# Layer-normalised tokens of two blocks turned by VectorE and DRAM instead of TensorE, in an attention-plus-GLU kernel

## The chip, the core and the metric

The kernel runs on one core of one Trainium2 chip. The core has a matrix engine (TensorE, PE in the profile, with its weight loads in a row of their own, PEld), a vector engine (VectorE, DVE), an activation engine (ScalarE, ACT), a general engine (GpSimd, POOL), and a queue engine (SyncE, SP) that here does nothing but issue DMA transfers. POOL issues a few transfers too. The metric is the time of one execution on the device in microseconds; the kernel before takes 676.23 us, the median of three executions (675.65 to 677.13).

## The reference

A layer normalisation feeds two branches, whose results are added to the input. One branch is attention with a compressive memory over four segments of 512 tokens, the other a gated feed-forward network. All is float32; there are 2048 tokens of 448 features, 16 heads of 28 features, and 1792 hidden units.

```python
xn = _layernorm(x, axis=-1)
return x + _A_ref(xn, A_wq, A_wk, A_wv, A_wo, A_beta) + _B_ref(xn, B_w_gate, B_w_up, B_w_down)

# _A_ref: q, k, v from xn; then, segment by segment (N = 4, L = 512)
logits = einsum("bhqd,bhkd->bhqk", qs, ks) * scale + mask
a_dot = einsum("bhqk,bhkd->bhqd", softmax(logits), vs)
pq = where(qs > 0, qs + 1, exp(qs))              # the same map of ks gives pk
a_mem = einsum("bhld,bhde->bhle", pq, M) / (einsum("bhld,bhd->bhl", pq, z)[..., None] + 1e-6)
o = g * a_mem + (1.0 - g) * a_dot                # g = sigmoid(beta), per head
M = M + einsum("bhld,bhle->bhde", pk, vs);  z = z + einsum("bhld->bhd", pk)
# then o @ wo
# _B_ref: (sigmoid(x @ w_gate) * (x @ w_up)) @ w_down
```

## The kernel before

**Blocks and parts.** The tokens are worked in four blocks `b` = 0 to 3 of 512 (`L`), each of four tiles `t` of 128 tokens. `acc[b]` holds a block's input as loaded, 128 tokens on the partitions, and later the sum that becomes the output. For the matrix products the normalised tokens are needed the other way round, features on the partitions: `xs[b]`, seven chunks of 512 tokens. To keep float32 accuracy on a faster number format, each operand is split in a rounded part (chunks 0 to 3 of `xs`) and what rounding left (chunks 4 to 6, and the upper 64 partitions of chunk 3, since 448 features fill three and a half chunks of 128). A product of two such operands is 11 matmuls, listed by chunk in `TERMS`.

**The front** is the first part of the program, about 155 us of it, and the only part in which the change moves compute work. For each block it makes values (`values`, four times 11 matmuls, into `pv`), then seven column groups `k` = 0 to 6 of keys and queries (`keys_queries`, 11 matmuls each into `pp`), which ACT copies and rounds, DVE subtracts (`qk`) and SP stores to DRAM (`qd`). Some groups also get their feature map (`e`, by ACT and DVE). At `k` = 2 to 5 the keys' feature maps are turned by PE (`key_rows`, into `pk`) and copied by ACT to `kn`; after `k` = 6 the memory is updated (`update`, into `pmm`). From block 2 on the memory is also recalled (`recall`, into four banks `n2`, by products with `phi`, which SP loads), turned back and divided by DVE (`answer`), and stored through POOL's queue (`od`).

**The next block's tokens** are prepared in between. `statistics` (DVE) and `root` (ACT, a square root, whose function table ACT has to load) give mean and scale; `normalise` (line 343, DVE) writes a tile to `xn`, and POOL copies its last 64 columns once more (line 351), so that the half chunk can serve for both parts; `turn` (line 354) has PE turn the tile by four matmuls against the identity (line 103, into a PSUM bank `pt`), ACT round it into `xs` (line 105), and DVE subtract (lines 110 and 111). Block 1's tiles are turned at `k` = 3 to 6 of block 0, and the tiles of blocks 2 and 3 at `k` = 1 to 4 of the block before. The token blocks 2 and 3 are loaded by SP, each in one transfer, during blocks 0 and 1 (line 588).

**What sets the order.** In the front the order on PE, ACT and DVE is that in which the code is written. SP and POOL are ordered by a planner in the front; every queue runs strictly in its order, so a transfer that waits holds back those behind it. The PSUM banks also set limits: `pp` alternates between two pairs of banks, the values use the pair `p` that the even groups of `pp` use, and a bank is free again when ACT and DVE have read it. From the end of the front on, the feed-forward network, the softmax attention and the output projection are woven into one PE stream in a fixed order (`MANUAL`), with `acc[b]` receiving the feed-forward results (`pd`).

## Time and profile before

The profile is of one execution, which took 674.82 us; its span, from the first instruction to the end of the last, is 673.0 us, so 1.82 us lie around it.

| | before |
|---|---|
| median of three executions | 676.23 us |
| the profiled execution | 674.82 us |
| its span | 673.0 us |
| PE busy | 666.4 us (99%) |
| DVE busy | 565.8 us (84%) |
| ACT busy | 338.3 us (50%) |
| POOL busy | 141.9 us (21%) |
| PE's share of the chain that ended last | 96% |
| granted TensorE clock | 1.00 |

How to read it: a "busy" time counts the moments in which an engine had at least one instruction at work. Matmuls are pipelined, so the duration of one (about 0.39 us for 128x512) is longer than the step from one to the next. The chain follows the program back from its last instruction, at each step to what released it, and gives each piece the time by which it moved the chain on; a stretch of four matmuls there is their real price. An instruction row in an answer by time has its start, the time that it or the merged run of its kind took, the engine and the line, and in brackets how long the engine had been idle and for what.

### The profile page before, as it was taken

How to read it: one execution, taken by the hardware profiler on the slowest of the kernel's cores; microseconds unless marked ns; L12 is line 12 of the kernel's file. 1: busy time of each engine (PE TensorE's matmuls, PEld its weight loads, DVE VectorE, ACT ScalarE, POOL GpSimd, SP SyncE). 2: the span in 40 equal slices, each digit the busy share in tenths (PEclk: the TensorE clock that was granted, in tenths of full speed). 3: DMA queues.
4: the chain of work that ended last, by engine and by line, in shares of the span. 5: the costliest groups of instructions: out<-in, count | busy, mean ns of one | idle time of the engine just before them, and what ended most of it. 6: DMA issues, size and time to landing. Idle time of an engine off the chain costs nothing.

```text
span 673.0 us, 11207 instructions
## 1 busy us (share of the span) xinstructions
PE 666.4 (99%) x3954; PEld 555.8 (83%) x3954; DVE 565.8 (84%) x987; ACT 338.3 (50%) x563; POOL 141.9 (21%) x346
## 2 busy tenths in 40 slices
PE   8999999999999999999999999999999999999997
PEld 7888878778878888887887888788787887888897
DVE  6765686668999899899998899899998998999864
ACT  5846564524455464555644555464545554545320
POOL 3500010002212222232221212222222221321000
PEclk9999999999999999999999999999999999999999
DMA  7446658894423234323346322425342332423342
GB/s 273 176 163 250 204 224 259 299 298 148 127 57 102 59 110 106 85 74 89 72 77 134 94 72 57 103 57 138 79 102 57 98 89 70 99 78 79 96 166 100
DMA packets 45919, 84.42 MB, mean 125 GB/s; under 512 B 6312, under 2 KB 20520, under 8 KB 45352
## 3 DMA queue, kind: packets, MB, share of 16 engines
q1 hardware_dynamic: 42712, 76.26, 38.2%
q0 software_dynamic: 3008, 7.34, 5.1%
q8 instruction: 31, 0.51, 0.3%
q14 instruction: 24, 0.20, 0.1%
q10 hardware_dynamic: 144, 0.11, 0.0%
HBM read 51.05 MB, written 32.64 MB: 124 GB/s over the span
## 4 chain that ended last, share of the span: by engine, by line
PE 96%; DVE 2%; issue 1%; ACT 1%; DMA 0%; DVEq 0%
PE pgu L255 42%; PE pd L181 20%; PE pp L380 10%; PE st L658 6%; PE pa L744 5%; PE po L843 5%; PE pv L360 4%; PE pt L103 1%; PE pk L402 1%; PE n L435 0%; DVE e L392 0%; PE pmm L413 0%; DMA acc<-in_x 0%; DVE stats L319 0%; DVE xn L345 0%
## 5 line engine op out<-in xcount | busy, mean ns | idle before, releaser
L255 PE MATMUL pgu<-xs,wgu 128*128 128x512 f32 x1232 | 301.3, 392 | 0.0
L255 PEld LDWEIGHTS pgu<-xs,wgu 128*128 128x128 f32 x1232 | 228.7, 188 | 46.7 <-issue 2.5
L181 PE MATMUL pd<-wdn,hh 128*128 128x448 f32 x672 | 155.3, 366 | 0.0
L181 PEld LDWEIGHTS pd<-wdn,hh 128*128 128x128 f32 x672 | 122.7, 188 | 11.6 <-issue 0.8
L673 POOL TENSOR_SCALAR_AFFINE_SELECT w<-w 128x256 f32<-128x256 f32 (+1 forms) x160 | 76.8, 483 | 217.8 <-ACT w L662 151.5
L726 ACT ACTIVATE w<-w 128x1024 f32<-128x1024 f32 (+1 forms) x96 | 87.9, 915 | 58.2 <-DVE w L722 58.2
L662 ACT ACTIVATE w<-st 128x512 f32<-128x512 f32 x128 | 75.6, 592 | 56.7 <-PE st L658 52.3
L722 DVE TENSOR_TENSOR w<-w,mb 128x1024 f32<-128x1024 f32 (+1 forms) x96 | 100.4, 1053 | 0.8
L680 DVE TRANSPOSE_TENSOR_REDUCE mx<-w 128x32 f32<-128x1024 f32 x64 | 78.9, 1233 | 4.0 <-POOL w L673 4.0
L380 PE MATMUL pp<-xs,wqk 128*128 128x512 f32 x308 | 75.8, 395 | 0.2 <-DVE kn L441 0.2
L278 ACT ACTIVATE hh<-sg 128x512 fp32r<-128x512 f32 x56 | 35.4, 631 | 71.6 <-DVE sg L272 50.3
L183 DVE TENSOR_TENSOR acc<-pd,acc 128x448 f32<-128x448 f32 x112 | 67.4, 602 | 4.0 <-PE pd L181 4.0
L380 PEld LDWEIGHTS pp<-xs,wqk 128*128 128x128 f32 x308 | 56.6, 188 | 12.6 <-issue 0.8
L658 PE MATMUL st<-qk 84*128 84x128 f32 (+3 forms) x256 | 62.0, 313 | 0.0
L658 PEld LDWEIGHTS st<-qk 84*128 84x128 f32 x256 | 47.9, 189 | 8.7 <-issue 1.4
L262 ACT ACTIVATE sg<-pgu 128x512 f32<-128x512 f32 x56 | 33.2, 592 | 40.8 <-PE pgu L255 40.8
L387 DVE TENSOR_TENSOR qk<-pp,qk 128x512 fp32r<-128x512 f32 x28 | 19.3, 689 | 32.8 <-ACT e L385 29.9
L272 DVE SCALAR_TENSOR_TENSOR sg<-sg,pgu 128x512 f32<-128x512 f32 x56 | 37.7, 673 | 9.3 <-PE pgu L255 9.3
L708 DVE STREAM_TRANSPOSE mb<-top 128x1024 f32<-128x1024 f32 x32 | 39.5, 1235 | 3.3 <-POOL top L705 3.2
L360 PE MATMUL pv<-wv,xs 128*128 128x448 f32 x176 | 37.7, 368 | 0.9 <-DVE e L392 0.5
L281 DVE SCALAR_TENSOR_TENSOR hh<-sg,hh 128x512 fp32r<-128x512 f32 x56 | 38.2, 682 | 0.3 <-ACT hh L278 0.3
L744 PE MATMUL pa<-w,vv 128*32 128x128 f32 (+3 forms) x512 | 37.8, 436 | 0.0
(100 smaller groups left out, 604.8 us busy)
## 6 DMA issues: line engine op xcount, KB each, us to landing
qk<-qd SPq DMA_DIRECT2D x192, 112.0 KB
qd<-qk SPq DMA_DIRECT2D x28, 512.0 KB
raw<-in_w_ffn SPq DMA_DIRECT2D x14, 512.0 KB
vd<-vst SPq DMA_DIRECT2D x4, 1024.0 KB
vv<-vd SPq DMA_DIRECT2D x16, 256.0 KB
od<-w POOLq DMA_DIRECT2D x16, 256.0 KB, 4.1
sums<-od SPq DMA_DIRECT2D x32, 128.0 KB
out<-acc SPq DMA_DIRECT2D x15, 224.0 KB
```

The source lines that it names most:

```text
L181: T.matmul(pd[:, :D], l, r, start=n == 0, stop=n == len(mms) - 1)
L183: V.tensor_add(acc[b][:, t, :], pd[:, :D], acc[b][:, t, :])
L255: T.matmul(dst, wgu[f][:, w, side * P:(side + 1) * P], xs[b][:, a, :], start=n == 0, stop=n == len(TERMS) - 1)
L360: T.matmul(pv[:, :D], xs[b][:, a, t * P:(t + 1) * P], wv[w], start=n == 0, stop=n == len(TERMS) - 1)
L380: T.matmul(pp, wqk[c][:, w, :], xs[b][:, a, :], start=n == 0, stop=n == len(TERMS) - 1)
L658: T.matmul(st[:, at:at + L - kb * P], self.qk[:KS, 1, h, kb * P:(kb + 1) * P], self.qk[:KS, 0, h, kb * P:], start=True, stop=True)
L662: A.activation(w, st, AF.Copy)
L673: G.affine_select(d, d, pattern=pattern, base=0, channel_multiplier=-1, compare_op=ALU.is_ge, fill=MASK)
L680: V.tensor_reduce(self.mx[:, 32 * h:32 * h + 32], w3[:, h, :2 * L].rearrange("p (b n) -> p b n", n=32), axis=mybir.AxisListType.X, op=ALU. ...
L722: V.tensor_sub(w, w, m)
L726: A.activation(w, w, AF.Exp, scale=SCALE)
L744: T.matmul(pa[32 * j:32 * j + 32, kb * P:], self.vv[:, kb, 32 * j:32 * j + 32], self.pairs[j // 2].block(j % 2, kb), start=kb == 0, stop=k ...
```

## The change

In blocks 2 and 3 PE no longer turns the tokens; blocks 0 and 1 stay as they were. The tokens of blocks 2 and 3 are loaded in another layout (`load_strips`): a strip of 32 partitions takes 128 neighbouring tokens, so that partition 32q + r of tile t holds token 128q + 32t + r. After `normalise`, DVE turns each tile in squares of 32 by 32 (`V.transpose`) into a stage, which is the memory of `phi` for block 2 and that of `acc[2]` for block 3. Then (`spread`) four SP transfers write the stage to a new DRAM tensor `xd[b]`, features by tokens, in runs of 128 tokens (512 bytes); POOL issues two transfers that read it back, three full chunks straight into `xs[b]` chunks 4 to 6, and the last 64 features into a tile `tail`. `split_strips` finally makes the two parts in SBUF: ACT rounds and DVE subtracts, a chunk at a time at `k` = 2 to 5 of the block before, where PE's turned tiles were split.

The work also moves in time. Block 2's strips are loaded right behind the first weights, block 3's after the first key group of block 0. Block 2's statistics are now taken before block 0's key groups, its first tile is normalised at `k` = 5 of block 0, its other three while PE makes block 1's values. Block 3's statistics follow there, and its four tiles are normalised at `k` = 0 to 3 of block 1. Because `acc[2]` and `acc[3]` then hold strips or a stage, both blocks are loaded once more in their old layout at the start of the feed-forward network. POOL's copy of the 64 columns is left out for blocks 2 and 3.

PE in block 1, around its key groups `k` = 1 to 4 (`pp`, 11 matmuls each); `pk` are the key rows, `pt` the turned tokens. Before:

```order
L380 MATMUL pp<-xs_66,wqk_115 128x512 x11
L103 MATMUL pt<-ident,xn 128x128 x4
L380 MATMUL pp<-xs_66,wqk_116 128x512 x11
L402 MATMUL pk<-ident,e 128x128 x4
L103 MATMUL pt<-ident,xn 128x128 x4
L380 MATMUL pp<-xs_66,wqk_117 128x512 x11
L402 MATMUL pk<-ident,e 128x128 x4
L103 MATMUL pt<-ident,xn 128x128 x4
L380 MATMUL pp<-xs_66,wqk_118 128x512 x11
```

And now:

```order
L415 MATMUL pp<-xs_66,wqk_119 128x512 x11
L415 MATMUL pp<-xs_66,wqk_120 128x512 x11
L437 MATMUL pk<-ident,e 128x128 x4
L415 MATMUL pp<-xs_66,wqk_121 128x512 x11
L437 MATMUL pk<-ident,e 128x128 x4
L415 MATMUL pp<-xs_66,wqk_122 128x512 x11
```

The fours of `pt` are gone, and nothing has come in their place; block 2 reads the same, and the rest of PE's order is as it was.

DVE at the end of block 0 and while PE makes block 1's values (`qk` is the subtraction of key group 6, `mst` the memory's update, `xs_66` block 1's last tile; `acc_71` is block 2, `phi` its stage). Now:

```order
L353 TENSOR_SCALAR xn<-acc_71,mv_348,y_520 128x16x7x4
L362 STREAM_TRANSPOSE phi<-xn 128x14x32
L422 TENSOR_TENSOR qk<-pp,qk 128x512
L455 COPY mst_126<-pmm 28x128 x4
L110 TENSOR_TENSOR xs_66<-pt,xs_66 128x3x128
L111 TENSOR_TENSOR xs_66<-pt,xs_66 64x128
L353 TENSOR_SCALAR xn<-acc_71,mv_348,y_520 128x16x7x4
L362 STREAM_TRANSPOSE phi<-xn 128x14x32
```

Before, the two rows ahead of `qk` and the two at the end were not there; block 2's statistics stood at the end, and its normalisation came later.

POOL around its last weight splits (`wqk`, the seven key and query weights) and its copies of 64 columns (`xn`). Before:

```order
L479 TENSOR_TENSOR wqk_119<-wqk_raw,wqk_119 128x512
L351 COPY xn<-xn 128x64
L479 TENSOR_TENSOR wqk_120<-wqk_raw,wqk_120 128x512
L351 COPY xn<-xn 128x64 x9
```

And now:

```order
L515 TENSOR_TENSOR wqk_123<-wqk_raw,wqk_123 128x512
L515 TENSOR_TENSOR wqk_124<-wqk_raw,wqk_124 128x512
L359 COPY xn<-xn 128x64 x4
L376 DMA xs_67<-xd_93 128x3x512
L378 DMA tail<-xd_93 64x512
```

The first copy, for block 1's first tile, has moved behind the last weight's split (wqk_120 before, wqk_124 now); the eight copies for blocks 2 and 3 are gone, and the read of block 2's turned tokens (xs_67, tail) follows.

The diff:

```diff
@@ -116,6 +116,11 @@
     def x_block(b):
         return x[b * L:(b + 1) * L, :].rearrange("(t p) d -> p t d", p=P)
 
+    def load_strips(b):
+        for q in range(4):
+            nc.sync.dma_start(acc[b][32 * q:32 * q + 32],
+                              x[b * L + q * P:b * L + (q + 1) * P, :].rearrange("(t r) d -> r t d", r=32))
+
     ps = ctx.enter_context(tc.tile_pool(name="psum", bufs=1, space=PSUM))
 
     banks = {"p": 2, "s": 2, "m": 1, "gu": 2, "pd": 1}
@@ -147,6 +152,7 @@
     qd = [dram.tile([2 * D, 2, L], F32, name=f"qd{b}") for b in range(NB)]
     fd = [dram.tile([D, L], F32, name=f"fd{b}") for b in range(NB)]
     vd = [dram.tile([P, NT, H * 32], F32, name=f"vd{b}") for b in range(NB)]
+    xd = [dram.tile([D, L], F32, name=f"xd{b}") for b in range(NB)]
     od = [dram.tile([H * 32, L], F32, name=f"od{b}") for b in range(NB)]
 
     mid = ctx.enter_context(tc.tile_pool(name="mid", bufs=3, reuse_waits="tile"))
@@ -227,6 +233,8 @@
             ahead = {}
             if f0 == 0:
                 ahead[0, 0] = lambda: (load_down(1, "raw"), ready_up(1))
+                ahead[0, 3] = lambda: nc.sync.dma_start(acc[2], x_block(2))
+                ahead[1, 1] = lambda: nc.sync.dma_start(acc[3], x_block(3))
                 ahead[0, 2] = lambda: load_up(2)
                 ahead[1, 3] = lambda: load_up(3)
             if f0 + FG < NF:
@@ -313,8 +321,8 @@
         def statistics(b, t0, steps):
 
             stats = sb.tile([P, steps, 6], F32, name=f"stats{steps}")
-            mv = sb.tile([P, steps, 2], F32, name=f"mv{steps}")
-            vh = sb.tile([P, steps], F32, name=f"vh{steps}")
+            mv = sb.tile([P, steps, 2], F32, name=f"mv{steps}", bufs=3)
+            vh = sb.tile([P, steps], F32, name=f"vh{steps}", bufs=3)
             for t in range(steps):
                 V.bn_stats(stats[:, t, :], acc[b][:, t0 + t, :])
                 V.bn_aggr(mv[:, t, :], stats[:, t, :])
@@ -347,9 +355,36 @@
                               op0=ALU.subtract, op1=ALU.mult)
             if b == 0:
                 A.activation(xn[:, D:], xn[:, 384:D], AF.Copy)
+            elif b == 1:
+                G.tensor_copy(xn[:, D:], xn[:, 384:D])
             else:
-                G.tensor_copy(xn[:, D:], xn[:, 384:D])
+                s3 = stage_of(b).rearrange("p (i n) -> p i n", n=P)
+                V.transpose(s3[:, :, 32 * t:32 * t + 32], xn[:, :D].rearrange("p (i r) -> p i r", r=32))
             return xn
+
+        def stage_of(b):
+            if b not in stages:
+                space = features() if b == 2 else acc[2]
+                stages[b] = space.rearrange("p t n -> p (t n)")[:, :NT * D]
+            return stages[b]
+
+        def spread(b):
+
+            for q in range(4):
+                nc.sync.dma_start(xd[b][:, q * P:(q + 1) * P].rearrange("(i c) n -> c i n", c=32),
+                                  stage_of(b)[32 * q:32 * q + 32].rearrange("c (i n) -> c i n", n=P))
+            nc.gpsimd.dma_start(xs[b][:, 4:7, :].bitcast(F32), xd[b][:384].rearrange("(k p) n -> p k n", p=P))
+            tail[b] = two_k("tail")
+            nc.gpsimd.dma_start(tail[b][:64], xd[b][384:])
+
+        def split_strips(b, k):
+
+            if k < 3:
+                A.activation(xs[b][:, k, :], xs[b][:, 4 + k, :].bitcast(F32), AF.Copy)
+                V.tensor_sub(xs[b][:, 4 + k, :], xs[b][:, 4 + k, :].bitcast(F32), xs[b][:, k, :].bitcast(F32))
+            else:
+                A.activation(xs[b][:64, 3, :], tail[b][:64], AF.Copy)
+                V.tensor_sub(xs[b][64:, 3, :], tail[b][:64], xs[b][:64, 3, :].bitcast(F32))
 
         def turn(b, t, xn):
             transpose_split(bank("pt", "s"), xn, xs[b], t)
@@ -370,7 +405,7 @@
             value_terms(b, t, pv, EARLY[1] if b == 0 else TERMS)
             store_values(b, t, pv)
 
-        stored = {}
+        stored, tail, stages = {}, {}, {}
 
         def keys_queries(b, c, between=None):
 
@@ -466,6 +501,7 @@
         with nc.allow_non_contiguous_dma(reason="a strip's heads"):
             for j in range(HG):
                 nc.sync.dma_start(gate[32 * j:32 * j + 32], beta[j::HG].partition_broadcast(32))
+        load_strips(2)
         G.memset(vst[:, :, :, DH:], 1.0)
         A.activation(gate_n, vst[:, 0, :NG, DH], AF.Sqrt)
 
@@ -543,23 +579,23 @@
                 phi = features()
                 for i in range(NG):
                     load_features(b - 1, i, phi)
-            st = None
             for t in range(3 if b == 0 else 0, NT):
                 values(b, t)
                 if b == 0:
                     split_qk(t)
-                if last:
-                    continue
-                if t == (3 if b == 0 else 0):
-                    mv, vh = statistics(b + 1, 0, NT)
-                if t == (3 if b == 0 else 0):
-                    st = mv, vh, root(vh)
-                if t == (3 if b == 0 else 2):
+                    mv, vh = statistics(1, 0, NT)
+                    st[1] = mv, vh, root(vh)
                     A.activation(one, ident[:, 0:1], AF.Exp)
-            if st and b > 0:
-                st = rstd(*st)
-                for n in range(2):
-                    xn[n] = normalise(b + 1, n, *st[n])
+                    st[2] = statistics(2, 0, NT)
+                if b == 1 and t < 3:
+                    normalise(2, t + 1, *st[2][t + 1])
+                if b == 1 and t == 2:
+                    spread(2)
+                    mv, vh = statistics(3, 0, NT)
+                if b == 1 and t == 3:
+                    st[3] = mv, vh, root(vh)
+                    A.activation(one, ident[:, 0:1], AF.Exp)
+                    st[3] = rstd(*st[3])
             e = {}
             for k, c in enumerate((3, 4, 5, 6, 0, 1, 2) if last else range(7)):
                 def recalled():
@@ -577,15 +613,15 @@
                     answer(b - 1, n - 1, ts)
                 if k == 0:
                     if b == 0:
-                        st = rstd(*st)
+                        st[1] = rstd(*st[1])
                     if b == 0:
                         A.activation(gate, gate, AF.Exp, scale=-1.0)
                         V.tensor_scalar_add(gate, gate, 1.0)
                         V.reciprocal(gate, gate)
                         V.tensor_scalar(gate_n, gate, -1.0, 1.0, op0=ALU.mult, op1=ALU.add)
-                if (b, k) in ((0, 3), (1, 0)):
+                if (b, k) == (0, 0):
                     with tc.issue_after(stored[b, c]):
-                        nc.sync.dma_start(acc[b + 2], x_block(b + 2))
+                        load_strips(3)
                 if (b, k) in ((2, 1), (3, 0)):
                     with tc.issue_after(stored[b, c]):
                         next(ffn)
@@ -604,11 +640,23 @@
                     key_rows(k - 2, e[k - 2])
                 if k == 6:
                     update(b)
-                n = k - 1 if b == 0 else k + 1
-                if 2 <= n < 6:
-                    turn(b + 1, n - 2, xn[n - 2])
-                if 0 <= n < 4 and n not in xn:
-                    xn[n] = normalise(b + 1, n, *st[n])
+                if b == 0:
+                    if 3 <= k:
+                        turn(1, k - 3, xn[k - 3])
+                    if 1 <= k < 5:
+                        xn[k - 1] = normalise(1, k - 1, *st[1][k - 1])
+                    if k == 4:
+                        y = root(st[2][1])
+                    if k == 5:
+                        st[2] = rstd(*st[2], y)
+                        normalise(2, 0, *st[2][0])
+                else:
+                    if 2 <= k < 6:
+                        split_strips(b + 1, k - 2)
+                    if b == 1 and k < 4:
+                        normalise(3, k, *st[3][k])
+                    if b == 1 and k == 3:
+                        spread(3)
                 if b == 2 and k == 6:
                     next(ffn)
             if last:
```

## The prediction

> **What bounds the kernel now.** I read the page's busy times first, then the chain that ended last.
>
> ```profile
> PE 666.4 (99%) x3954; PEld 555.8 (83%) x3954; DVE 565.8 (84%) x987; ACT 338.3 (50%) x563; POOL 141.9 (21%) x346
> ...
> PE 96%; DVE 2%; issue 1%; ACT 1%; DMA 0%; DVEq 0%
> ```
>
> PE works for all but 6.6 us of the span of 673.0, and the chain lies on it for 96%: what PE no longer has to do is worth its own time, as long as nothing else becomes late. The chain by time, in block 1, gives the price of a turned tile:
>
> ```profile
> 56.03 0.44 PE pt L103 x4
> 56.47 2.52 PE pp L380 x11
> 59.00 0.44 PE pk L402 x4
> ```
>
> Four matmuls of line 103 move the chain on by 0.44 us. (The 270 ns or so that a single one lasts overlaps its neighbours and is not the price.) The third view is the busy time by block; the rows end where PE begins the values of blocks 1, 2 and (late, see below) 3:
>
> ```profile
> core 0: us, PE busy (x) PEld busy (x) DVE busy (x) ACT busy (x) POOL busy (x), PEclk, DMA share, GB/s
> 0.00:42.20 42.20, 39.80 (x328) 34.09 (x329) 29.59 (x75) 26.32 (x55) 15.47 (x22) 1.00 0.64 231
> 42.20:73.40 31.20, 31.20 (x283) 26.89 (x281) 18.70 (x43) 20.80 (x38) 1.10 (x4) 1.00 0.53 196
> 73.40:109.30 35.90, 35.33 (x325) 29.19 (x325) 29.39 (x66) 22.76 (x40) 3.49 (x8) 1.00 0.63 223
> ```
>
> Block 1 (second row) has PE without a gap and DVE with 12.5 us free. In block 2 (third row) DVE is at 82%, and there PE does wait, at its end:
>
> ```profile
> 106.28 2.48 PE L360 MATMUL pv<-wv,xs 128*128 128x448 f32 x11
> 109.28 1.08 PE L360 MATMUL pv<-wv,xs 128*128 128x448 f32 x4 [0.52 <-DVE e L392]
> ```
>
> The second value tile of block 3 needs a PSUM bank that DVE's last feature map of block 2 still reads. Without gaps the eleven matmuls from 106.28 would hand over about 2.2 us later, at 108.5, so 0.8 us are lost there, and DVE sets the pace of block 2.
>
> **PE's part: what is removed.** Eight fours of 0.44 us, four in block 1 and four in block 2: 3.5 us. Nothing is added on PE. In block 1 PE alone sets the pace, so its four are worth 1.75 us.
>
> **DVE's part.** The rows of DVE's kinds in the front:
>
> ```profile
> L319 DVE BATCH_NORM_STATS2 stats<-acc 128x6 f32<-128x448 f32 x16 | 9.7, 607 | 3.3 <-DMA acc<-in_x 3.2
> L345 DVE TENSOR_SCALAR xn<-acc,mv,y 128x448 f32<-128x448 f32 x16 | 8.9, 564 | 0.6
> L110 DVE TENSOR_TENSOR xs<-pt,xs 128x384 fp32r<-128x384 f32 x16 | 8.7, 547 | 2.5 <-ACT xs L105 2.4
> L111 DVE TENSOR_TENSOR xs<-pt,xs 64x128 fp32r<-64x128 f32 x16 | 4.7, 294 | 0.3
> L446 DVE STREAM_TRANSPOSE tb<-phi 128x512 f32<-128x512 f32 x4 | 2.8, 711 | 0.1
> L94 DVE TENSOR_TENSOR wgu<-raw,wgu 128x1024 fp32r<-128x1024 f32 x1 | 1.2, 1228 | 0.0
> ```
>
> A tile's turn in squares has 448 of the 512 columns of line 446: 0.62 us. Its output is scattered in runs of 32, which no row shows; I bound it by 0.62 and, at twice that, 1.25, and take 0.62, since line 446 moves the same squares. A chunk's split in SBUF is half of line 94: 0.61 us, against 0.55 + 0.29 = 0.84 for a tile's split now.
> - Block 2 loses four splits of 0.84 and two normalisations of 0.56 and gets four splits of 0.61: 3.36 + 1.13 - 2.44 = 2.0 us less. DVE paces that block, so PE's wait for the bank ends 2.0 us earlier: this, not PE's 1.75, is block 2's gain.
> - Block 1 gets three more normalisations (seven instead of four, 1.7), seven turns (4.3), and saves 0.9 on splits: 5.1 us more, 23.8 in a stretch of 29.45. Free time covers it; if it did not, each us over would be a us on PE.
> - Block 0 gets statistics (four times 0.61, and as much again by a quarter for the aggregation, 3.1), a scale (an estimated 0.7, four short instructions), one normalisation and one turn: about 5 us, 34.6 of the first row's 42.2. Nothing taken but a push on POOL's copy, below.
>
> **POOL's queue.** It was passed by one step: the copy for block 1's first tile now stands behind the last weight split.
>
> ```profile
> 28.96 0.62 ACT L478 ACTIVATE wqk<-wqk_raw 128x512 fp32r<-128x512 f32 x1
> 29.38 0.24 POOL L351 COPY xn<-xn 128x64 f32<-128x64 f32 x1 [0.59 <-DVE xn L345]
> 29.66 1.28 POOL L479 TENSOR_TENSOR wqk<-wqk_raw,wqk 128x512 fp32r<-128x512 f32 x1
> 30.45 0.60 PE L103 MATMUL pt<-ident,xn 128*128 128x128 f32 x4
> ```
>
> ACT's part ends at 29.58, the split 1.28 later at 30.86, the copy at 31.10. PE needs it for the fourth matmul of the group, at 30.45 + 0.33 = 30.78: a new wait of 0.3 us (bounds 0 and 0.5, with DVE's push). PE is queued behind it with block 0's keys.
>
> **The trip of block 2 through DRAM** is the one new long wait. ACT reads the returned chunk at block 1's `k` = 2, behind the copy of the key rows; behind ACT's wait stand its `pp` copies, and for these PE waits.
>
> ```profile
> 43.49 0.29 DVE L111 TENSOR_TENSOR xs<-pt,xs 64x128 fp32r<-64x128 f32 x1
> ...
> 54.69 0.69 DVE L387 TENSOR_TENSOR qk<-pp,qk 128x512 fp32r<-128x512 f32 x1 [5.57 <-ACT e L385]
> ...
> 61.17 0.59 ACT L105 ACTIVATE xs<-pt 128x512 fp32r<-128x512 f32 x1
> ...
> 73.99 0.69 DVE L392 SCALAR_TENSOR_TENSOR e<-pp,e 128x512 f32<-128x512 f32 x1
> ...
> 75.83 0.55 ACT L364 ACTIVATE vst<-pv 128x448 f32<-128x448 f32 x1 [1.88 <-PE pv L360]
> ```
>
> Departure: DVE's work for block 1 ends at 43.8 plus 0.2; three normalisations and turns of 1.18 follow: 47.6. Due: 61.17 less one four that PE no longer makes, 60.7. Beyond it, the last bank of the block is now freed at 74.7 and first needed by the second value tile at about 75.7, so 1.0 us of lateness costs nothing. The way, from the DMA rates by stretch and the landing of POOL's transfers of 256 KB:
>
> ```profile
> 15.00:21.00 6.00, 6.00 (x33) 5.38 (x32) 4.83 (x13) 4.02 (x8) 3.65 (x3) 1.00 0.05 7
> 52.00:55.00 3.00, 3.00 (x15) 2.48 (x14) 0.31 (x1) 1.39 (x3) 0.00 (x0) 1.00 0.85 350
> 147.00:151.00 4.00, 4.00 (x19) 3.34 (x18) 2.20 (x4) 1.06 (x2) 0.00 (x0) 1.00 0.91 177
> 196.50:197.50 1.00, 1.00 (x6) 0.81 (x6) 1.00 (x2) 0.69 (x2) 0.29 (x1) 1.00 1.08 216
> ...
> L447 POOL DMA_DIRECT2D od<-tb x12: 539/539/747, 93.5 to 162.4; - x12
> ...
> DMA to landing us min/median/max: 2.3/2.7/5.2
> ```
>
> In the first the queues are all but empty (used below); the second moves the value store (128 partitions, long runs), the third loads of `qk` (28 partitions, 2 KB), the fourth loads of `vv` (512-byte runs). The write is 0.92 MB in 512-byte runs from 32 partitions: 4.3 us at 216 GB/s, 5.2 at 177. A transfer's fixed part is 2.3 - 0.75 (256 KB at 350 GB/s) = 1.5 us at least, at most 5.2 - 0.75 = 4.4. The write lands at 53.4 to 54.3. The read of 0.79 MB takes 2.2 us at 350 GB/s, or 4.4 when it shares with the value store, plus 1.5 to 4.4: back at 57.1 to 63.1, in the middle 60.1. I take no wait; the late end, 63.1, would cost 63.1 - 60.7 - 1.0 = 1.4 us.
>
> **Covered at nothing.** Block 3's trip leaves at `k` = 3 of block 1 and is due at `k` = 2 of block 2, some 25 us for 10 to 15. The strips for block 2 are due when DVE has taken block 1's statistics, at about 21; the queues are empty from 15 (share 0.05 in the row above), and 0.92 MB take 2.6 to 5.2 us at 350 and 177 GB/s. ACT's splits replace its equal `xs` rows; its root and table loads (1.28 us each) only move. The second loads of `acc`, 1.8 MB, are issued by SP at about 154, ahead of a weight load and of this:
>
> ```profile
> 167.24 2.47 SPq L640 DMA_DIRECT2D qk<-qd  x6
> ```
>
> These transfers wait for PE until 167, so the 5 to 10 us of loading (at 350 and 177 GB/s) lie in a free stretch; without it they would push the weight load.
>
> **The sum**, for the profiled execution (674.82 = 673.0 + 1.82 around): -1.75 (block 1) - 2.0 (block 2) + 0.3 (POOL's copy) = -3.45, to 671.4. The median shown is 1.41 above that execution: 672.8.
>
> **Rivals.**
> - Late return, part of the gain lost. For it: the due time lies inside my bounds. Against: their middle is before it. 0.2 to 1.4 us lost: 673.0 to 674.2.
> - POOL issues the read late, because DVE holds it up. POOL's landings spread by 5.2 - 2.3 = 2.9 us; on top of the middle, 60.1, that is 63.0, and 1.3 us are lost: 674.1. Against: the issue is due at 53.4 to 54.3, when DVE, done with block 3's statistics by about 51 and with its scale by 52.6, waits for the first key group (54.69 in the row); and POOL's issues last 0.54 to 0.75 us though DVE is 82% busy there. The Trainium skill (SBUF — State Buffer, SBUF: two separate sides) has the rule behind this rival: a transfer issued by POOL, 620 ns alone, took 3100 beside a DVE copy, since POOL could not write its descriptors. By that figure the read would be an estimated 2.5 us late, and 0.9 us lost; the trace's issue rows do not show it.
> - DVE becomes block 1's bound because scattered turns cost 1.25. A key group at `k` = 2 and 3 then has 0.69 + 0.68 + 0.61 + 0.56 + 1.25 = 3.8 us of DVE against 2.96 of PE, on top of a departure 1.9 later. The later groups give 0.9 back each. About 1.5 to 2 us lost: 674.5.
> - Slower: the write of block 2. If short runs and few partitions multiply (350 to 216, and 350 to 177), it moves at 109 GB/s and takes 8.4 us; with 1.5 to 4.4 of fixed part each way the trip ends at 61.2 to 69.2. ACT stands, PE with it. Each us beyond 61.7 costs one, and from 65.15 the kernel is slower. At the late end it costs 7.5: 680.3; a typical such case, 67, gives 678. For it: no row has both traits. Against: such a case needs the slowest value for each step.
> - No change: PE's freed time turns into waits elsewhere in the front, for instance if the strips came late. Against: every queue has the slack above. 675.5 to 677.
>
> **How the numbers follow.** Forecast 0.62 (its own range 671.8 to 673.8), late return 0.09, POOL held up 0.04, DVE 0.07, slower 0.11, no change 0.07. A measurement of this kernel can tell about 0.2%, 1.35 us, from no change. Faster by more (below 674.9): 0.62 + 0.09 + 0.04 + 0.04 (part of the DVE case) = 0.79. Slower (above 677.6): 0.10, the last 0.01 of that case staying below. Within: 0.11. The range, 671.3 to 676.0, takes in the late return, POOL's and DVE's cases and the near half of no change, and leaves the slower one out.
>
> **What would show it.** Right: no `pt` in blocks 1 and 2, PE gapless from the start of block 1's values to block 2's, the block-3 values starting 3 to 4 us earlier, turns of 0.6 us, a first split in block 1 that waits for no transfer, and everything after the front merely shifted. Wrong: ACT idle ahead of that split for POOL's read, followed by PE; turns of over 1 us; PE waiting in block 0 for more than 0.5 us at block 1's first tile; gaps for `raw` after 155 us.

## The result, and the profile after

The changed kernel takes 684.64 us, the median of six executions (682.78 to 686.15); the kernel before, on the same chip, 676.12 us, also of six (675.65 to 677.13). The ratio is 1.012 with an interval of 1.0101 to 1.0139: it is slower by 1.2%, where the forecast had it faster by 0.5%, and 684.64 lies above the range (671.3 to 676.0). The profiled execution took 682.8 us with a span of 681.0.

The page of the changed kernel: busy time of PE, the granted clock in 40 slices of 17.0 us, and the chain that ended last by engine.

```profile
PE 670.1 (98%) x3922; PEld 554.1 (81%) x3922; DVE 567.8 (83%) x987; ACT 335.9 (49%) x560; POOL 142.7 (21%) x342
...
PEclk9999969999999999999999999999999999999999
...
PE 86%; DMA 8%; DVE 2%; ACT 2%; issue 1%; SPq 0%; DVEq 0%; POOL 0%; POOLq 0%; ACTq 0%
```

PE has 32 matmuls less and is busy 3.7 us longer. Two things are new: DMA holds 8% of the chain (0% before), and the clock, at 9 in every slice before, has a 6 in the sixth, at 85 to 102 us. By places, from the starts of the same instructions in both traces:

| stretch | before, us | after, us | difference | forecast |
|---|---|---|---|---|
| start to block 1's values | 41.97 | 43.25 | +1.28 | +0.3 |
| to block 2's values | 31.35 | 30.15 | -1.20 | -1.75 |
| to the second value tile of block 3 | 35.96 | 42.69 | +6.73 | -2.0 |
| to the first scores | 45.41 | 45.92 | +0.51 | 0 |
| to the end of the span | 518.31 | 518.99 | +0.68 | 0 |

The third row is the loss. The chain of the changed kernel by time (start, us by which the chain moved on) shows where it lies:

```profile
56.84 7.75 DMA xs<-xd
...
64.62 0.02 ACT xs L383
...
73.96 5.50 DMA fd<-e
...
79.54 7.99 DMA phi<-fd
...
87.58 5.24 PE n L470 x32
92.82 7.38 PE pp L415 x22
```

Read from the end. The recall (`n`, 32 short matmuls in block 2's first key group) needs `phi`, block 1's query features, which ACT and DVE make (`e`), SP stores to DRAM (`fd`) and loads again in another layout. The second of its four stores is issued at 73.96 and has landed 5.5 us later, the first load takes 8.0, and at 87.58 PE may go on. In the chain the store hangs on ACT, and ACT on the strips of block 2, back from DRAM at 64.60; the timeline corrects the first of these two links. The rows of SP and PE before:

```profile
72.17 0.61 SPq L428 DMA_DIRECT2D phi<-fd  x1
74.71 1.41 SPq L395 DMA_DIRECT2D fd<-e  x1
76.17 2.89 SPq L428 DMA_DIRECT2D phi<-fd  x3
...
84.84 1.22 PE L435 MATMUL n<-phi,mst 28*32 28x512 f32 x32
85.99 2.80 PE L380 MATMUL pp<-xs,wqk 128*128 128x512 f32 x11
```

and after, with those of VectorE that complete the second and the last `e`:

```profile
69.98 3.29 SPq L374 DMA_DIRECT2D xd<-acc  x4
...
73.96 1.29 SPq L430 DMA_DIRECT2D fd<-e  x1
...
78.94 0.41 SPq L430 DMA_DIRECT2D fd<-e  x1
79.54 7.50 SPq L463 DMA_DIRECT2D phi<-fd  x4
...
70.45 0.68 DVE L427 SCALAR_TENSOR_TENSOR e<-pp,e 128x512 f32<-128x512 f32 x1
...
74.62 0.69 DVE L427 SCALAR_TENSOR_TENSOR e<-pp,e 128x512 f32<-128x512 f32 x1
...
87.58 5.24 PE L470 MATMUL n<-phi,mst 28*32 28x512 f32 x32 [2.61 <-DMA phi<-fd]
92.75 7.45 PE L415 MATMUL pp<-xs,wqk 128*128 128x512 f32 x22
```

Before, three of the four loads were issued between 76.17 and 79.06, five us or more ahead of the recall. After, the second `e` is ready at 71.13 and the last at 75.31 (0.6 us later than before), but SP is busy with block 3's strips (`xd<-acc`, from 69.98) and with the stores that queue up after these, and the two go out 2.8 and 3.6 us late, at 73.96 and 78.94. The four loads follow between 79.54 and 87.04. Their row is long because SP waits in it, 5.5 us in all, for stores of `e` to land. So SP's queue and the late landing delay the loads; ACT's lag adds little to it directly. PE idles 2.61 us, then gets one load after the other: the recall lasts from 84.97 to 92.82, 7.85 us, where it moved PE on by 1.15 before (84.84 to 85.99). Behind it the 22 matmuls of the next two key groups take 7.38 us on the chain. Windows of the changed kernel show why (the columns are the busy time of PE, PEld, DVE, ACT, POOL, then the granted clock, the DMA share and GB/s):

```profile
83.75:87.10 3.35, 1.22 (x6) 0.68 (x4) 0.69 (x1) 1.72 (x3) 0.00 (x0) 1.00 0.96 307
87.15:97.30 10.15, 9.72 (x43) 4.40 (x44) 3.11 (x5) 0.00 (x0) 0.00 (x0) 0.50 0.62 203
```

From 87.15 to 97.30 the clock is 0.50, right behind a stretch in which PE worked 1.22 of 3.35 us, and in that stretch the DMA engines were busy for 96%. At full clock the same 22 matmuls move PE on by 5.1 us (in the last kernel below, 85.08 to 90.21), so the clock costs 2.2 us here and the wait 6.7. The rest of block 2 is 2.2 us shorter than before.

My theory ahead of the experiments, which still followed the chain: the loss is made at the recall. Block 3's trip puts its 1.8 MB between the stores of `e` and the loads of `phi`, and block 2's late strips hold ACT up ahead of the same stores; PE's wait for `phi` then halves its clock. The rivals: that the late strips of block 0 start it, that block 2's late trip alone does, or that the clock falls for a reason of its own.

### The profile page after: what moved, and what is told of

The parts are those of the page before. It is cut to its first block, busy times and chain, and to the rows that moved or that the text cites. A ratio compares the mean times of both kernels' runs of the same rounds, so it can differ in the third digit from the quotient of the medians.

```text
span 681.0 us, 11171 instructions
## 1 busy us (share of the span) xinstructions
PE 670.1 (98%) x3922; PEld 554.1 (81%) x3922; DVE 567.8 (83%) x987; ACT 335.9 (49%) x560; POOL 142.7 (21%) x342
## 4 chain that ended last, share of the span: by engine, by line
PE 86%; DMA 8%; DVE 2%; ACT 2%; issue 1%; SPq 0%; DVEq 0%; POOL 0%; POOLq 0%; ACTq 0%
PE pgu L263 41%; PE pd L187 20%; PE pp L415 6%; PE st L706 6%; PE pa L792 5%; PE po L891 5%; DMA wqk_raw<-in_w_qk 1%; DMA phi<-fd 1%; DMA xs<-xd 1%; PE n L470 1%; PE pv L395 1%; DMA acc<-in_x 1%; DMA od<-w 1%; DMA fd<-e 1%; DMA xd<-phi 1%
## 5 line engine op out<-in xcount | busy, mean ns | idle before, releaser
L415 PE MATMUL pp<-xs,wqk 128*128 128x512 f32 x308 | 77.2, 403 | 0.2 <-DVE kn L476 0.2
L415 PEld LDWEIGHTS pp<-xs,wqk 128*128 128x128 f32 x308 | 58.4, 193 | 14.0 <-issue 1.7
```

Source lines behind the costliest of these rows:

```text
L415: T.matmul(pp, wqk[c][:, w, :], xs[b][:, a, :], start=n == 0, stop=n == len(TERMS) - 1)
```

## The experiments

All times are medians; the ratio is to the kernel before on the same chip.

### Block 2's strips ahead of the gate's loads

```diff
+        load_strips(2)
         with nc.allow_non_contiguous_dma(reason="a strip's heads"):
             for j in range(HG):
                 nc.sync.dma_start(gate[32 * j:32 * j + 32], ...)
-        load_strips(2)
```

> Edit: the four loads of block 2's strips are issued ahead of the four loads of the gate (the sync queue's order alone). Theory A (the loads of phi for block 2's recall come late behind a backlog of DMA traffic, PE waits for them, and the waits bring the granted clock down to 0.5): VectorE no longer waits for the strips at 23 us, the first values of block 1 come at about 42.0 instead of 43.25 us, and everything behind moves with them, the recall's wait and the half clock stay: about 684.6 - 1.3 = 683.3 us. Rival B (the late strips of block 0 set the lag of ScalarE that makes the keys' stores, and with them phi, late): the recall's wait goes with them, 675 to 678 us.

684.5 us, ratio 1.0131 (1.0104 to 1.0158): nothing gained, where theory A had 1.3 us. VectorE's wait for the strips is gone and block 1's values start at 42.67 instead of 43.25, but the recall's wait has grown by more (rows of this run's timeline):

```profile
31.45 0.33 PE L103 MATMUL pt<-ident,xn 128*128 128x128 f32 x1 [0.40 <-POOL xn L359]
88.11 5.38 PE L470 MATMUL n<-phi,mst 28*32 28x512 f32 x32 [3.53 <-DMA phi<-fd]
```

When PE gets there does not matter; `phi` sets the time. This strikes out the strips of block 0 as the cause. The first row is POOL's copy behind the last weight split, 0.40 us where I had forecast 0.3.

### Only block 2 through DRAM

Block 3 is loaded and normalised as before and turned by PE; there is no third trip.

```diff
-                        load_strips(3)
+                        nc.sync.dma_start(acc[3], x_block(3))     # at (1, 0)
...
-                    if b == 1 and k == 3:
-                        spread(3)
+                    if b == 2 and 1 <= k < 5:
+                        turn(3, k - 1, xn[k - 1])
```

> Edit: block 2 keeps the way through VectorE and DRAM, block 3 is loaded, normalised and transposed by PE as in the kernel before, so that there is no third trip (0.92 MB written and read between 70 and 84 us) beside the keys' stores and the loads of phi. Theory A with that trip as the cause of the backlog: phi lands some 7 us earlier, the recall in block 2 starts without a wait of over 1 us, the clock stays at 1.0; 684.6 - 8.9 for the recall + 1.6 for the fours of transposes that come back into block 2 = about 677.3 us. Rival B (the lag of ScalarE, that block 2's late trip leaves, is the cause): wait and half clock stay, 684.6 + 1.6 = about 686 us. In between if both have a share.

681.2 us, ratio 1.0077 (1.0062 to 1.0092), between the two expectations. In the timeline:

```profile
67.70 0.63 ACT L382 ACTIVATE xs<-xs 128x512 fp32r<-128x512 f32 x1 [4.99 <-DMA xs<-xd]
88.40 1.22 PE L469 MATMUL n<-phi,mst 28*32 28x512 f32 x32
```

At the recall theory A holds: no wait, 1.22 us, and a clock of 1.0 throughout the profiled execution (two of the four had 0.997 in the mean). But block 2's trip is even later (ACT waits until 67.70; block 3's tokens are loaded from 57.71 on beside it), and PE, after waits of 1.53 and 1.11 us in block 1, reaches the recall 3.4 us later than in the changed kernel. So this run takes the third trip away and makes the second worse.

### Block 2's recall two groups later

```diff
-                e[c] = keys_queries(b, c, recalled if b > 1 and n == 0 else None)
+                e[c] = keys_queries(b, c, recalled if b > 1 and n == (2 if b == 2 else 0) else None)
```

with the answers at groups 3 to 6 and the recall's banks in an order that suits.

> Edit: block 2's recall, its transposes and answers stand two key groups later (behind group 2 instead of group 0); the traffic stays as it is. PE then reaches the recall about 4.7 us later, at 89.7 us instead of 85.0 at full clock, while the last load of phi lands at about 92. Theory A (wait and clock drop at this one place): less wait by 4.7 us, the gap of 2.6 us ahead of the first load gone, and with it most of the half clock: 676 to 679 us. Rival C (the clock drop comes from something else in this stretch, e.g. from the work itself): only the wait gets shorter, 680 us or more.

679.28 us, ratio 1.0056 (1.0034 to 1.0077): 5.4 us are back, just short of the expectation, without any change of traffic. The profiled execution was the slowest of the four (682.05); in the fastest (678.54) the mean clock was 1.0. In the profiled one the first half of the recall runs without a wait, at 90.32, and the clock still falls, for a shorter time (windows, columns as above):

```profile
90.30:93.60 3.30, 2.82 (x33) 0.48 (x32) 0.80 (x2) 1.72 (x3) 0.00 (x0) 1.00 1.06 331
93.70:100.40 6.70, 5.93 (x19) 4.45 (x16) 3.76 (x6) 1.11 (x2) 0.00 (x0) 0.50 0.89 350
```

The first row's 2.82 us of PE mislead: the 32 short matmuls wait for two loads between each other, and the weight loads, 0.48 us, show how little was done. A thin stretch of this kind is enough for half the clock.

### Work for PE while it waits

```diff
             for i in range(NG):
+                for _ in range((12 if i == 0 else 3) if b == 1 else 0):
+                    T.matmul(n2[i], wqk[0][:, 0, :], xs[2][:, 0, :], start=True, stop=True)
```

> Edit: 12 matmuls of 128x512 (some 2.6 us, into the bank that the recall overwrites next) are put ahead of block 2's recall, and 3 ahead of each of its other three parts, so that PE has work while it waits for phi; nothing else is changed. If the waits are what brings the clock down: the loads land as before, the recall still ends at about 92.8 us, but the granted clock stays at 1.0, and the two key groups behind it (22 matmuls in 7.45 us at half clock, 4.65 us at full) gain about 2.8 us, the rest of the half-clock stretch some 0.3: about 681.5 us. If the clock drop has another cause (the DMA traffic, the heat of the stretch before): still half clock, 684.6 us or a little more.

686.42 us, ratio 1.0152 (1.0106 to 1.0198): by the time a miss, since the theory had 681.5. In the profiled execution its first half holds: with PE busy the clock stays. The window, and the row of the two groups in the timeline:

```profile
87.15:97.30 10.15, 10.15 (x57) 4.70 (x56) 2.64 (x5) 0.00 (x0) 0.00 (x0) 1.00 0.66 210
```

```profile
94.57 5.29 PE L415 MATMUL pp<-xs,wqk 128*128 128x512 f32 x22
```

The DMA engines were as busy as in the changed kernel (0.66 in this window, 0.62 there), so at this place idleness brought the clock down, and neither the traffic nor the work did. As a cure it is worth nothing: the fill ends the recall at 94.57 instead of 92.75, which eats most of the gain at the two groups, and the second value tile of block 3 starts at 115.81 against 116.09. The profiled execution (684.59) then loses 2.2 us at 172 us, by a wait that the part on the second loads treats. Two of the four executions, 688.24 and 689.71, had a mean clock of 0.992 in spite of the fill; where it fell in them no trace shows.

### Block 3's trip behind the loads of phi

```diff
-                    if b == 1 and k == 3:
-                        spread(3)
...
+                if b == 2 and t == 0:
+                    with tc.issue_after(loaded):      # the last load of phi
+                        spread(3)
```

> Edit: block 3's trip (four writes of strips and two reads) is issued behind the four loads of phi instead of ahead of three of the keys' stores; all else as in the changed kernel. Theory A with the third trip as the cause: phi lands before PE needs it or at most 1 us after, the clock stays at 1.0, block 3's strips are back by about 100 us and are split from about 95 us on behind the recall: 675.5 to 677 us. Rival B (lag of ScalarE from block 2's late trip): phi is still some 3 to 4 us late, the gap and the half clock stay in part: 680 to 684 us.

683.37 us, ratio 1.0114 (1.0097 to 1.0131): by the number a miss for theory A. The timeline says otherwise (SP, POOL, then PE):

```profile
81.76 3.10 SPq L374 DMA_DIRECT2D xd<-acc  x4
...
97.40 0.76 POOL L376 DMA_DIRECT2D xs<-xd  x1
...
85.18 1.25 PE L470 MATMUL n<-phi,mst 28*32 28x512 f32 x32
106.30 1.09 PE L437 MATMUL pk<-ident,e 128*128 128x128 f32 x4 [5.79 <-DVE rc L145]
```

The recall starts at 85.18 without a wait, although block 2's trip is as late as ever (ACT's first split at 64.90): with the third trip out of the way the last `e` goes out at 75.62, the loads from 76.21 on, and ACT's lag by itself does the recall no harm. The time is lost 20 us later. POOL's read of block 3's strips got its place behind two of the answers' stores, was issued at 97.40, and PE waited 5.79 us for VectorE, which waited for the strips; half the clock followed, from 102.55 to 109.25 us.

### The reads on the sync engine

Two runs from this: block 2's reads by SP with the third trip left where it was, and block 3's reads by SP with its trip behind `phi` and its splits at `k` = 3 to 6.

```diff
-            nc.gpsimd.dma_start(xs[b][:, 4:7, :].bitcast(F32), xd[b][:384]...)
+            back = nc.sync if b == 2 else nc.gpsimd       # b == 3 in the second run
+            back.dma_start(xs[b][:, 4:7, :].bitcast(F32), xd[b][:384]...)
```

> Edit: the two reads of block 2's trip are issued by the sync engine, behind block 1's value store, instead of by GpSimd; the third trip stays as it is. Block 2's strips, back at 64.6 us in the changed kernel, should come back up to 3 us earlier. If the lateness of this trip (through ScalarE's lag and the keys' stores) makes phi late, the recall's wait shrinks by as much, and with it the half clock: 677 to 681 us. If the third trip's traffic makes phi late, as the run with that trip behind phi says: phi lands when it did, 683.5 to 685 us.

681.45 us, ratio 1.0077 (1.0055 to 1.0100), 0.45 above the first expectation. Block 2's strips are split from 61.98 on instead of 64.62, without a wait of ACT, and no gap is left in block 1. The third trip and the recall in the timeline:

```profile
67.42 2.77 SPq L374 DMA_DIRECT2D xd<-acc  x4
...
76.92 7.68 SPq L464 DMA_DIRECT2D phi<-fd  x4
...
85.09 1.97 PE L471 MATMUL n<-phi,mst 28*32 28x512 f32 x16 [0.73 <-DMA phi<-fd]
...
90.14 7.08 PE L416 MATMUL pp<-xs,wqk 128*128 128x512 f32 x22
```

It runs from 84.36 to 90.14, 5.8 us instead of 7.85, and the clock still halves. The late second trip has a share, 3.2 us of the time; the larger part stays. Its way to `phi` is the third trip: this one leaves 2.6 us earlier than in the changed kernel (67.42 for 69.98), and so does the first load of `phi` (76.92 for 79.54). Block 3's last turn stands behind block 2's splits on VectorE, so a late second trip makes the third leave late.

> Edit: block 3's trip behind the loads of phi as in the run before of that kind, but its two reads are issued by the sync engine directly behind the writes and the values' store, not by GpSimd between two of the answers' stores, and block 3's strips are split at groups 3 to 6 instead of 2 to 5. Theory: that run lost its gain only to the late read (issued at 97.4 us, back at 103, PE waiting 5.8 us at 100 to 106 us and the clock at half for 6.8 us behind it); with the read at about 90 us it is back at about 97, the first split at about 98, no wait of over 0.7 us in blocks 2 and 3, the clock at 1.0 throughout, the second value tile of block 3 at about 108: 674.5 to 676 us. If GpSimd was not what held the read, the wait stays: 681 to 683 us.

679.57 us, ratio 1.0047 (1.0022 to 1.0073), between the two expectations. No wait at the recall and none at 100 us, so POOL's place was what held the read (the splits also stand a group later here; in the last kernel of the next part, with the old splits, nothing waits at 100 us either). What remained was of my making: with the last split at `k` = 6, VectorE did it behind the memory's update, and block 3's values waited (timeline):

```profile
107.07 0.47 PE L396 MATMUL pv<-wv,xs 128*128 128x448 f32 x1 [0.62 <-DVE xs L385]
110.08 8.72 PE L396 MATMUL pv<-wv,xs 128*128 128x448 f32 x35 [2.54 <-DVE xs L388]
```

### All three orders together

Strips first, all reads by SP, block 3's trip behind `phi`; splits at `k` = 3 to 6.

> Edit: the three orders together: block 2's strips ahead of the gate's loads, both trips' reads from the sync engine, block 3's trip behind the loads of phi with its splits at groups 3 to 6. By the terms: 674.5 to 676 us of the run with the third trip moved, less 0.6 us in block 0 and up to 0.5 us where PE waited for the keys' transposes at the end of block 1: 673.5 to 675 us. If the sync engine, waiting for the write of block 2's strips, holds up the stores behind it so that key tiles run out of buffers, 676 us or more.

678.41 us, ratio 1.0024 (1.0001 to 1.0046), over the forecast of 673.5 to 675, with the same two waits (0.51 and 2.54 us) and a stretch of half clock behind them. With the splits back at `k` = 2 to 5:

> Edit: the three orders together again, but block 3's strips are split at groups 2 to 5 as in the changed kernel, not at 3 to 6. In the run with all three, the strips were back by about 92 us (the last 2 KB packets of their reads run at 91 to 92), while the last split stood behind the memory's update on VectorE at 108.05 us, and PE waited 0.51 and 2.54 us for the splits at 105 to 109 and lost 3.4 us at half clock behind them. Theory: both waits and the half clock go: 677.5 (its profiled execution) - 3.05 - 1.7 = about 672.7 us in a profiled execution, 672.5 to 675 us as a median. If VectorE is the bound of block 2 (95% busy at 93 to 100 us in the profile of the kernel before), the splits only move its wait into the keys' terms: 676 us or more.

674.49 us, ratio 0.9974 (0.9957 to 0.9992): as expected, and faster than the kernel before. In the profiled execution both waits are gone and the clock is 1.0 throughout; two of the twelve had a mean of 0.997. The second value tile of block 3 starts at 106.48, 2.8 us ahead of the kernel before; in the medians 1.7 of these are left.

### The third trip's traffic alone, in the kernel before

```diff
+                if b == 1 and k == 3:
+                    ...     # four writes acc[3] -> xd[3] in 512-byte runs, two reads qd[0] -> xs[3]
```

The copied data are used by nothing.

> Edit: the kernel before, unchanged in its work, with the third trip's traffic alone added at group 3 of block 1: four writes of 224 KB in runs of 512 bytes out of the tokens' tile of block 3 to a scratch tensor in DRAM, and two reads of 768 and 128 KB in runs of 2 KB into block 3's operand space that is overwritten later. Nothing waits for them. If the third trip's 1.8 MB delay phi by themselves (at some 290 GB/s, 6.3 us): PE waits 1 to 3 us at block 2's recall, the granted clock falls to 0.5 there: 679 to 684 us. If the lag of ScalarE is needed as well: no wait of over 0.7 us and a clock of 1.0 in block 2, 676 to 677.5 us.

679.25 us, ratio 1.0047 (1.0027 to 1.0066): at the low edge of the first expectation. In the timeline of the profiled execution (677.92 us):

```profile
79.40 4.53 SPq L429 DMA_DIRECT2D phi<-fd  x4
...
85.63 2.73 PE L436 MATMUL n<-phi,mst 28*32 28x512 f32 x32
```

The last load is out at 83.9 instead of 79.1, and the recall takes 2.73 us instead of 1.22, its waits between the four loads. The clock held in that execution, one of the fastest of the ten; six of the others had a mean of 0.995 or 0.997. So this traffic costs 3.0 us by itself, half clock included, in a kernel that has no second trip. That the changed kernel loses more fits the two runs above: with block 2's trip early it is 3.2 us less, with the third trip behind `phi` the recall waits for nothing.

### The second loads of the tokens

In the kernel with all orders VectorE waits at the end of the front for the buffer of an answer's store, and PE for VectorE (timeline):

```profile
161.15 0.71 DVE L482 STREAM_TRANSPOSE tb<-kn 128x512 f32<-128x512 f32 x1 [4.22 <-DMA od<-tb]
...
162.43 1.48 PE L187 MATMUL pd<-wdn,hh 128*128 128x448 f32 x6 [1.84 <-DVE acc L189]
```

The second loads of `acc[2]` and `acc[3]` are issued at 151.6 to 152.8 there. Two runs move them from FFN steps (0, 3) and (1, 1) to (2, 0) and (3, 0), in that kernel and in the changed one.

> Edit: the same, and the second loads of the last two blocks' tokens (0.92 MB each, issued at 155 to 161 us in the runs so far) stand two FFN steps later. Theory: at 160 to 170 us they delay the answers' stores, VectorE waits for a buffer of these (2.8 us in the changed kernel, 3.5 us in the run with the fill), and PE in some executions for VectorE (2.2 us there, 0.3 us in the changed kernel): 0.3 to 2 us less than the run beside it, 672 to 674 us, with less scatter. If the stores are late for another reason: the same as the run beside it within 0.3 us.

674.1 us, ratio 0.9978 (0.9960 to 0.9995), against 674.49: not to be told apart. The profiled execution was one of the slowest of its twelve (677.44): VectorE waited 1.69 us for an answer's store at 100 us, and block 3's values for VectorE (timeline):

```profile
107.36 0.67 PE L396 MATMUL pv<-wv,xs 128*128 128x448 f32 x2 [1.22 <-DVE xs L388]
108.68 8.47 PE L396 MATMUL pv<-wv,xs 128*128 128x448 f32 x33 [0.65 <-DVE e L428]
```

A stretch of half clock followed. So the orders keep block 3 free of the waits in most executions, not in all: three of the twelve here had a mean clock of 0.997.

> Edit: the changed kernel, with the second loads of the last two blocks' tokens two FFN steps later and nothing else. By the same theory 0.3 to 2 us less than the changed kernel's 684.6 us, by how many executions lose PE's wait at 170 us: 682.5 to 684.3 us. If these loads do no harm: 684.6 us.

684.31 us, ratio 1.0113 (1.0090 to 1.0136): the same as the changed kernel. Neither run answers the question: the first of the two loads was still issued at 155.6 and 161.3 us, among the answers' stores, because nothing ahead of it in SP's queue waits. Moved to (2, 1) and (3, 1), both stand behind loads that wait for PE:

```diff
-                ahead[0, 3] = lambda: nc.sync.dma_start(acc[2], x_block(2))
-                ahead[1, 1] = lambda: nc.sync.dma_start(acc[3], x_block(3))
+                ahead[2, 1] = lambda: nc.sync.dma_start(acc[2], x_block(2))
+                ahead[3, 1] = lambda: nc.sync.dma_start(acc[3], x_block(3))
```

> Edit: the kernel with the three orders and splits at groups 2 to 5, and both second loads of the last two blocks' tokens moved behind the attention's loads that wait for PE until 167 us or later (in the last try the first of the two was still issued at 155.6 us, ahead of them, so that PE's wait of 1.2 us at 165 us was no answer). Theory: these 1.8 MB, in rows of 1792 bytes at 154 to 162 us, hold up the answers' stores (VectorE waits 4.2 us for one) and PE by 1.8 us at 162 us; behind 167 us they hold up nothing: VectorE's wait falls to the 1.2 us of the kernel before, PE's is gone, the end comes some 519 us after the first scores instead of 521.4: 672 to 673.5 us as a median. If other loads (weights, the twelve of the attention) hold up the stores: the wait of 1 to 2 us stays, 674 to 675 us.

673.94 us, ratio 0.9965 (0.9952 to 0.9979): the lowest median, yet above the first expectation (672 to 673.5) and just below the second. Its six executions lie within 1.5 us (673.18 to 674.69), where the twelve of the run without this edit spread over 4.3.

```profile
156.85 0.71 DVE L482 STREAM_TRANSPOSE tb<-kn 128x512 f32<-128x512 f32 x1 [1.79 <-DMA od<-tb]
```

and from its page:

```profile
PEclk9999999999999999999999999999999999999999
...
PE 93%; DVE 2%; issue 1%; POOL 1%; ACT 0%; DMA 0%; DVEq 0%; POOLq 0%; ACTq 0%
```

VectorE's wait is 1.79 us (forecast: 1.2), PE's is gone, and from the first scores to the end it takes 518.65 us, as before (518.31). The medians of this run and the one without the edit differ by less than their intervals; that the loads cause the wait rests on the rows of one execution each.

> Edit: the changed kernel with the second loads moved in the same way and nothing else. By the same theory 0.3 us (its profiled execution) to 2 us (executions with PE's wait at 170 us) less than 684.6 us: 682.7 to 684.3 us; otherwise 684.6 us.

683.5 us, ratio 1.0105 (1.0090 to 1.0120), inside the expectation, and 1.1 us under the changed kernel's median of another set of executions: a small part of its loss, if any.

## Why the prediction was wrong

- **Where it failed.** "Covered at nothing. Block 3's trip leaves at `k` = 3 of block 1 and is due at `k` = 2 of block 2, some 25 us for 10 to 15." Its own due time was met: ACT's first split of it, at 102.36, waits for no transfer. I did not ask what it delays: between its departure and its due time block 1's features go to DRAM and come back as `phi`, which the recall needs at 85 us, and in the kernel before the last of its loads was issued only 5.8 us ahead of the recall. The four writes of the strips stand ahead of three of these stores in SP's queue, and the strips' bytes share the DMA engines with stores and loads. This omitted wait (6.7 us), made worse by the trip of block 2, and the half clock behind it (2.2) are 8.9 us. None of the rivals has that place; the slower one has a late write of block 2, but with ACT and PE standing in block 1.
- **Block 2's trip came back later than my late end.** It left at 48.93 for 47.6 (block 0's delay); the write took until 56.14 by the chain, 7.2 us for 5.8 to 6.7; the read 7.75, inside 3.7 to 8.8; back at 64.60 for 57.1 to 63.1. The timeline of the changed kernel:

```profile
48.26 0.65 DVE L362 STREAM_TRANSPOSE phi<-xn 128x448 f32<-128x448 f32 x1
48.93 3.04 SPq L374 DMA_DIRECT2D xd<-phi  x4
56.84 0.96 POOL L376 DMA_DIRECT2D xs<-xd  x1 [18.52 <-DMA xd<-phi]
...
64.62 0.63 ACT L383 ACTIVATE xs<-xs 128x512 fp32r<-128x512 f32 x1 [2.54 <-DMA xs<-xd]
...
72.50 0.97 PE L448 MATMUL pmm<-vst,kn 128*28 128x32 f32 x90 [0.39 <-ACT kn L439]
```

  My rule "each us beyond costs one" was too harsh on the spot: 3.9 us beyond the due time cost PE 0.39 in block 1, since ACT caught up. The larger cost came through the third trip, which left late behind it. POOL's issue (0.96 us, begun 0.7 after the landing) was not held up for the 2.5 us that the rival on VectorE and POOL allowed, though VectorE, which I had taken to be waiting, was at work from 55.98 on.
- **Block 1's four fours: right.** -1.75 forecast; in the kernel with all orders and late second loads block 1 takes 29.54 us instead of 31.35, -1.8. In the changed kernel it is -1.2; of the missing 0.6 the wait above explains 0.39.
- **Block 2, paced by VectorE: right in mechanism, its size between.** -2.0 forecast; from block 2's values to the second value tile of block 3 the two reordered kernels that keep the clock take 33.90 and 34.46 us instead of 35.96: -2.1 and -1.5. The wait for the bank remains (0.48 and 0.64 us), as it should. My list for VectorE counted two of four normalisations that leave the block and none of its statistics; the others lay ahead of the key groups, in VectorE's idle time, and change nothing.
- **The turn in squares: right.** 0.62 forecast, 0.65 in the row above; the scattered output costs next to nothing, and the rival built on 1.25 falls.
- **Block 0: under-sized.** +0.3 for POOL's copy, which shows with the strips first (0.40); in the changed kernel an earlier wait of PE (0.79, below) leaves it no room. The strips came late ("the queues are empty from 15", and the strips due at about 21): SP issued their loads from 12.34 on, behind the gate's, which had taken 4.27 us to issue. The timeline of the changed kernel:

```profile
22.99 0.63 DVE L327 BATCH_NORM_STATS2 stats<-acc 128x6 f32<-128x448 f32 x1 [1.57 <-DMA acc<-in_x]
28.09 0.66 PE L437 MATMUL pk<-ident,e 128*128 128x128 f32 x4 [0.79 <-DVE e L427]
```

  Block 0 loses 1.28 instead of 0.3 us; with the strips ahead of the gate's loads it is 0.7 to 1.1. What else than POOL's copy makes these up was not traced.
- **The second loads: a size taken at nothing.** I looked at the next loads in SP's queue, which do wait until 167 us. The answers' stores of the last block, on POOL's queue, were the ones in the way: 1.84 us of PE in one reordered execution, 0.5 to 2.2 in others.
- **What the terms are worth where nothing collides**: by the spans, -1.6 us in the last kernel (671.4 against 673.0): +0.9 in block 0, -1.8, -1.5, +0.5 in block 3, +0.3 behind. By the medians -2.4, where the forecast, which put all orders at nothing, had -3.45.

## What to carry to other kernels

A transfer that is moved into a free-looking stretch has two prices: whether it is back in time, and which later transfer of the same queue or the same engines now comes behind it; list every load on which PE waits between its start and its end, with the slack of each. A wait of PE of two us or more costs more than itself when the clock falls behind it: 2.2 us here on top of 6.7. And when an edit is taken back by an order, look at the trace and not at the time alone: two of the runs here (the trip behind `phi`, its reads by SP) gained at the right place and lost it at a new one.

## What the runs showed of the hardware

- **The clock falls after some two us without work.** In five kernels the clock was 1.00 in one stretch and 0.50 in the next, with PE idle for 2.61 us (the changed kernel), 3.53 (strips first), 5.79 (the trip behind `phi`) or 2.54 (the late split), or only working through the 32 short matmuls with gaps of up to 1.3 us between the loads (recall two groups later). It does not wait for a gap's end: by finer windows it fell an estimated 2.1 us into the gap in the changed kernel (0.73 in the mean from 87.00 to 87.25, 0.50 behind that) and 2.0 us into that of 5.79 (0.97 from 102.25 to 102.50, 0.50 behind that). In the kernel with all orders and later loads, gaps of 1.22 and 0.65 us close together were enough; in the kernel with only block 2 through DRAM, gaps of 1.53 and 1.11 us some 4 us apart left it at 1.0. The half-clock stretches lie between 3.2 and 3.6, 6.7 and 7.0, and 10.15 and 10.3 us by the windows: one, two and three times some 3.4 us. The Trainium skill (TensorE: Matmul & The Clock Gate, What's actually happening) gives a free-running window of 3413 ns, which agrees with these lengths. The Trainium skill's rule that a whole idle window is needed, put as "no PE-idle gaps >~3.4µs" (TensorE: Matmul & The Clock Gate, HAM oscillation — how this bites in real kernels), does not agree: the window ahead of the fall had 1.22 us of matmuls in 3.35.
- **On loaded DMA engines a store lands late, and its reload with it.** SP issues one load of `phi` in 0.31 to 0.38 us in the changed kernel and in 0.32 to 0.61 before; what grows is the wait for the stores of `e`. The last two loads go out when the last store has landed, at 86.30 in the changed kernel and at 78.30 before. From the issue of that store (78.94 and 74.71) this is 7.4 us and 3.6. The share of the DMA engines from 70 to 80 us was 0.92 against 0.70, and from 80 to 91 us 0.93 against 0.48 (windows of the changed kernel, columns as above):

```profile
70.00:80.00 10.00, 9.61 (x169) 8.49 (x168) 6.02 (x12) 5.62 (x12) 1.30 (x2) 1.00 0.92 263
80.00:91.00 11.00, 8.39 (x52) 4.78 (x54) 0.69 (x1) 2.81 (x5) 0.00 (x0) 0.82 0.93 288
```

- **The time of a kernel with such a wait scatters, and the clock with it.** The run with all orders and late splits lies between 675.0 us, at a mean clock of 1.0, and 682.7, at 0.992; the last kernel, where PE waits for no transfer, between 673.2 and 674.7, at 0.999 to 1.0. By the lengths above, one stretch of 3.4 us at half clock is an estimated 0.0025 of the mean over 680 us, so 0.992 stands for three.
